# Causal masks as affine selects on GpSimd, with key copies and weight loads reordered, in a fused attention and MLP kernel

## The chip, the cores and the metric

The kernel runs on one core of a Trainium2 chip. The metric is the device time of one execution in microseconds. All profiles are of one execution on that core. The core has TensorE (PE, with its weight loads as PEld), VectorE (DVE), ScalarE (ACT), GpSimd (POOL) and SyncE (SP); loads are issued from the queues of SP, ACT and POOL.

## What is computed

Causal attention with 16 extra "beacon" keys and values that every query sees, for 8 batches and 8 heads of 576 positions and 64 features; then a two-layer network with a leaky ReLU on the 4608 x 512 result.

```
B, H, S, Nb, D = (8, 8, 576, 16, 64)
k_all = concatenate([beacon_k, k], axis=2);  v_all = concatenate([beacon_v, v], axis=2)
scores = 1/sqrt(D) * q @ k_all^T
causal[:, Nb:] = triu(ones((S, S)), k=1)
a = softmax(where(causal, -1e9, scores))
x = (a @ v_all).transpose(0, 2, 1, 3).reshape(B * S, H * D)
h = x @ w_in            # 512 x 2048
out = maximum(0.01 * h, h) @ w_out   # 2048 x 512
```

Inputs and output are fp32; the kernel computes in bf16 with fp32 sums.

## The kernel before, in words

**Units of work.** Two heads make a pair; there are 4 pairs per batch and 32 in all, numbered g. The 592 keys (16 beacons, then 576) lie in 5 chunks of up to 128 rows. For a pair, `score` multiplies key chunks with all queries that may see them, in four parts n = 0 to 3, and ScalarE takes the exponential of each part into a buffer `aT` (keys by queries; three buffers, used by g modulo 3). The score accumulators in PSUM are two, so part n waits until the exponential of part n - 2 has read its own. `masks` then sets to zero what a query may not see: only a triangle in the diagonal block of each chunk. Before the change, it multiplies the block by a 0/1 triangle `tri` on VectorE, in three instructions (lines 326, 333, 339). `value` multiplies `aT` by the values, which carry a column of ones for the row sums, in two halves; VectorE divides by the sums (lines 376, 377). `finish` transposes the result on TensorE, and VectorE copies it into `xT` (line 394).

**The network.** A chunk is 512 of the 4608 rows, so there are 9. `moe1` makes one 128-column slice of the hidden layer of a chunk: 4 matmuls (line 403) and a leaky ReLU on ScalarE (line 410). `moe2` makes a quarter of one output tile: 4 matmuls (line 425), and with the fourth quarter a VectorE copy and a store. Each such set of 4 matmuls is called a group; there are 288. `fill` issues the next group that may be issued: a chunk's first layer once `ready` says that its rows are finished, and second-layer groups in turn with them.

**Keys and queries.** They come in by loads with a cast to bf16, on GpSimd's queue (`load_qk`, 4 loads per half batch, line 149). For batches 0 and 1 (pairs 0 to 7) `t_q` transposes them on TensorE; VectorE copies the queries, ScalarE the keys (line 264; for pair 3 VectorE copies both). The first pair has its own fp32 loads (`load_first_pair`, into a `v_raw` buffer). For batches 2 to 7, `permute` reorders them on GpSimd (line 178), `turn_pairs` transposes them by DMA on SP's queue (line 276), and `in_order` puts them in order on GpSimd (lines 289, 291), one pair ahead. From pair 9 on, an edge added by hand (`behind`) makes `in_order` for pair g + 1 wait for the masks of pair g - 1. Beacon keys are cast by `cast_beacon_k` (line 191), transposed by `beacon_transposes`, and copied in front of each key tile.

**Values.** `load_v` brings a batch in as fp32 on SP's queue (lines 224, 227, 229; two buffers), and `cast_v` casts it on GpSimd, chunk by chunk (line 238).

**Weights.** `load_w_in` and `load_w_out` bring each matrix in with a cast on GpSimd's queue, in four pieces of 512 KB each (bf16), after the loads and casts of batches 0 and 1.

**Order.** The order on each engine is the order of the program's text (`manual_schedule`); nothing is moved by a scheduler. Step g of the main loop issues `loads(g)`, scores of pair g, values of pair g - 2, and `finish(g - 3)`. In steps 0 to 7 the attention of batches 0 and 1 stands alone, with three fills in steps 6 and 7. At g = 8 the rest of these pairs is drained with 27 fills, and from then on each step spreads its share of the remaining groups over eight slots between the attention's parts.

Of the kernel before, what the change touches and what calls it, by code (L numbers as in the profile page):

```python
# [15 lines left out]
def kernel(  # L16
# [66 lines left out]
    tri = singles.tile([128, 128], BF16, name="tri")  # L83

    def make_mask():

        nc.gpsimd.memset(tri, 1.0)
        nc.gpsimd.affine_select(
            out=tri,
            in_=tri,  # L90
            compare_op=ALU.is_ge,
            fill=0.0,
            base=0,
            channel_multiplier=-1,
            pattern=[[1, 128]],
        )
# [25 lines left out]
    def load_w_in(i):  # L122
        return nc.gpsimd.dma_start(
            out=w_in_sb[:, :, i * 512 : (i + 1) * 512], in_=w_in_r[:, :, i * 512 : (i + 1) * 512]
        )

    def load_w_out(i):
        return nc.gpsimd.dma_start(
            out=w_out_sb[:, i * 4 : (i + 1) * 4, :], in_=w_out_r[:, i * 4 : (i + 1) * 4, :]
        )  # L130
# [27 lines left out]
    def load_first_pair():  # L158
        load_beacon_k(0, 1, nc.scalar)
        t = rawpool.tile([128, NKB, H, D], FP32, name="v_raw")  # L160
        flat = t[0:RP].rearrange("p c h d -> p (c h d)")
        n = 2 * RI * D
        for i in range(2):
            first_raw.append(flat[:, i * n : (i + 1) * n].rearrange("p (h i d) -> p h i d", h=2, i=RI))
        for eng, src, dst in zip((nc.sync, nc.scalar), (q, k), first_raw):
            last = eng.dma_start(out=dst, in_=src[0, 0:2].rearrange("h (p i) d -> p h i d", i=RI))
        return last
# [156 lines left out]
    def masks(g):  # L324
        aT = probs[g]
        nc.vector.tensor_tensor(
            out=aT[:, :, 0:112],
            in0=aT[:, :, 0:112],
            in1=tri[:, None, 16:128].to_broadcast([128, 2, 112]),
            op=ALU.mult,  # L330
        )
        diag = aT[:, :, 512 : 512 + 3 * 464].rearrange("p e (c x) -> p e c x", c=3)[:, :, :, 0:128]
        nc.vector.tensor_tensor(  # L333
            out=diag,
            in0=diag,
            in1=tri[:, None, None, :].to_broadcast([128, 2, 3, 128]),
            op=ALU.mult,
        )
        return nc.vector.tensor_tensor(  # L339
            out=aT[0:80, :, 1648:1728],  # L340
            in0=aT[0:80, :, 1648:1728],
            in1=tri[0:80, None, 0:80].to_broadcast([80, 2, 80]),
            op=ALU.mult,
        )
# [94 lines left out]
    done1, done2, ready, turn = [0], [0], [0], [0]  # L439

    def fill():
# [3 lines left out]
        can2 = i2 < NCH and i2 < i1  # L445
# [30 lines left out]
    with order:  # L476
# [4 lines left out]
        load_beacon_k(1, B, nc.sync)  # L481
        load_v(0, after=first)
        load_v(1)
        make_pads()
        make_mask()
        make_ones()
        cast_beacon_k(0, 1, nc.scalar.copy)
        nc.vector.tensor_copy(out=first_cast[0], in_=first_raw[0])
        nc.scalar.copy(out=first_cast[1], in_=first_raw[1])
        cast_beacon_k(1, B, nc.gpsimd.tensor_copy)  # L490
        cast_v(0, nc.gpsimd, 0, 2)
        load_qk(1, 0)
        cast_v(0, nc.gpsimd, 2, 5)
        load_qk(1, 1)
        load_w_in(0)
        cast_v(1, nc.gpsimd, 0, 3)
        load_w_in(1)
        cast_v(1, nc.gpsimd, 3, 5)
        for i in range(2, 4):
            load_w_in(i)  # L500
        for i in range(4):
            load_w_out(i)
        warm_up(34)
        beacon_transposes(0, 1)
# [3 lines left out]


        masked = {}  # L510

        def loads(g):
            b, hp = divmod(g, NPAIR)
            if g == 3:
                load_qk(2, 0)
            elif g == 5:
                load_qk(2, 1)
                for which in range(2):
                    permute(2, 0, which)
                turn_pairs(2, 0)  # L520
            elif g == 7:
                for which in range(2):
                    permute(2, 1, which)
                turn_pairs(2, 1)
                load_v(2)
                in_order(g + 1)
                cast_v(2, nc.gpsimd)
            elif g >= 2 * NPAIR:
                if has(g + 1):
                    copy = in_order(g + 1)  # L530
                    if g > 2 * NPAIR:
                        behind(copy, masked[g - 1])
# [27 lines left out]
        for g in range(NG + 3):  # L560
# [3 lines left out]
            if g < 2 * NPAIR:  # L564
# [5 lines left out]
                if g == 2:  # L570
                    beacon_transposes(1, B)
                if g + 1 < 2 * NPAIR:
                    t_q(g + 1, 0)
                    t_q(g + 1, 1, nc.vector.tensor_copy if g == 2 else nc.scalar.copy)
                if g > 2:
                    value(g - 2, 0)
                if g == 7:
                    fill()
# [4 lines left out]
                if g >= 6:  # L583
                    fill()
                if has(g - 2):
# [4 lines left out]
            if g == 2 * NPAIR:  # L590

                finish(g - 3)
                value(g - 2, 0)
                fill()
                value(g - 2, 1)
                fill()
                finish(g - 2)
                value(g - 1, 0)
                fill()
                value(g - 1, 1)  # L600
                fill()
                fill()
                finish(g - 1)
                for n in range(22):
                    fill()
# [35 lines left out]
            if has(g):  # L641
                masked[g] = masks(g)
# [33 lines left out]
```

## Time and profile before

| | |
|---|---|
| median of 11 runs | 357.91 us |
| lowest and highest | 355.52 and 360.32 us |
| the profiled execution | 357.29 us |
| its span in the profile | 355.6 us |
| mean granted TensorE clock | 0.981 |
| chain that ended last: PE, DMA, POOL | 70%, 15%, 6% |
| ScalarE exponentials (line 320), 128 | 104.3 us busy |
| VectorE masks (lines 326, 333, 339), 96 | 11.1 + 21.2 + 9.1 us busy |
| GpSimd key and query copies (line 291), 48 | 28.4 + 28.3 us busy |

The profile is of one execution. Its page gives the busy time of each engine, then the span in 40 equal slices with one digit of busy share for each, then groups of equal instructions by line: count, busy time, mean duration in ns, and the engine's idle time just ahead of them with what ended it. A line such as `A <- B: 1.3, 2, 0.8` among the waits means that A idled for B, in total 1.3 us, 2 times, at longest 0.8 us. "Granted clock" is the share of full speed that TensorE was given.

### The profile page before, as it was taken

Reading aid. Unit: us, or ns where it says so; the run is one execution under the profiler, and the core shown is the slowest. Engines: PE = TensorE matmul, PEld = TensorE weight load, DVE = VectorE, ACT = ScalarE, POOL = GpSimd, SP = SyncE. Lnnn points to the kernel's source line nnn. Section 1 sums busy time; section 2 is a strip of 40 time slices with the busy share of each in tenths; the row PEclk is TensorE's granted clock in tenths of the full one; section 3 lists DMA queues with packets and bytes.
Section 4 is the critical chain, followed back from the end, with each engine's and each line's share of the span. In section 5 each row is a group of like instructions: output and inputs, shape, how many; then the busy total and the mean of one; then the engine's idle time right before and its main releaser. Section 6 shows DMA issues by size and latency. Waiting matters only on the chain.

```text
span 355.6 us, 7310 instructions
## 1 busy us (share of the span) xinstructions
PE 340.3 (96%) x3002; PEld 172.2 (48%) x3002; DVE 123.5 (35%) x323; ACT 190.9 (54%) x282; POOL 153.3 (43%) x217
## 2 busy tenths in 40 slices
PE   5898899999899999999999999999999999999995
PEld 4476554444454444444444454444444554444444
DVE  2498630133656424322333234323332331000111
ACT  3989754476455873478436843685358304633300
POOL 7555516497698675745474547452220000000000
PEclk9589999999999999999999999999999999999999
DMA  8998999997997884993579355900110011000021
GB/s 163 204 209 134 193 196 193 207 219 122 179 225 130 168 152 107 117 231 54 96 143 225 59 98 95 194 3 0 61 60 2 2 63 55 2 29 29 31 78 71
DMA packets 86929, 40.87 MB, mean 115 GB/s; under 512 B 69872, under 2 KB 82160, under 8 KB 86896
## 3 DMA queue, kind: packets, MB, share of 16 engines
q1 hardware_dynamic: 73456, 26.75, 34.7%
q0 software_dynamic: 13152, 13.34, 25.1%
q10 hardware_dynamic: 288, 0.33, 0.4%
q8 instruction: 23, 0.38, 0.4%
q14 instruction: 10, 0.08, 0.1%
HBM read 37.22 MB, written 9.44 MB: 131 GB/s over the span
## 4 chain that ended last, share of the span: by engine, by line
PE 70%; DMA 15%; POOL 6%; issue 2%; DVE 2%; ACT 2%; SPq 2%; POOLq 0%
PE acc L425 30%; PE acc L403 27%; PE av L367 6%; DMA v_raw<-in_v_dram 6%; PE sc L311 5%; DMA w_out_sb<-in_moe_w_out_dram 4%; DMA q_raw<-in_q_dram 4%; DMA v_raw<-in_k_dram 1%; POOL qT L291 1%; PE tp L389 1%; DVE osb L434 1%; SPq L229 1%; ACT aT L320 1%; POOL kT L291 1%; POOL k_nat L178 1%
## 5 line engine op out<-in xcount | busy, mean ns | idle before, releaser
L403 PE MATMUL acc<-xT,w_in_sb 128*128 128x512 bf16 x576 | 140.2, 379 | 1.4 <-DVE xT L394 1.4
L425 PE MATMUL acc<-w_out_sb,gT 128*128 128x512 bf16 (+1 forms) x592 | 139.6, 374 | 0.0
L320 ACT ACTIVATE aT<-sc 128x1024 bf16<-128x1024 f32 (+3 forms) x128 | 104.3, 870 | 62.1 <-PE sc L311 62.0
L410 ACT ACTIVATE gT<-acc 128x512 bf16<-128x512 f32 x144 | 85.9, 601 | 80.1 <-PE acc L403 80.1
L425 PEld LDWEIGHTS <-gT 128*128 128x128 bf16 x592 | 53.3, 98 | 58.7 <-issue 6.1
L403 PEld LDWEIGHTS <-w_in_sb 128*128 128x128 bf16 x576 | 51.9, 98 | 59.5 <-issue 4.2
L434 DVE COPY osb<-acc 128x512 f32<-128x512 f32 (+1 forms) x37 | 25.1, 677 | 121.4 <-PE acc L425 121.4
L367 PEld LDWEIGHTS <-aT 128*128 128x128 bf16 (+1 forms) x960 | 37.4, 98 | 15.1 <-issue 3.3
L311 PE MATMUL sc<-qT,kT 64*128 64x80 bf16 (+4 forms) x384 | 37.3, 296 | 5.4 <-ACT aT L320 2.5
L367 PE MATMUL av<-v_aug,aT 128*128 128x65 bf16 (+1 forms) x960 | 40.6, 195 | 0.3 <-issue 0.3
L289 POOL COPY kT<-bkT 128x16 bf16<-128x16 bf16 x24 | 4.9, 206 | 63.4 <-DVE aT L339 63.4
L377 DVE TENSOR_TENSOR x_nat<-av,rec 128x384 bf16<-128x384 f32 x64 | 31.4, 491 | 2.2
L376 DVE RECIPROCAL rec<-av 128x6 f32<-128x6 f32 x64 | 12.0, 187 | 57.6 <-PE av L367 57.5
L238 POOL CAST v_aug<-v_raw 128x512 bf16<-128x512 f32 (+1 forms) x40 | 23.8, 629 | 18.0 <-DMA v_raw<-in_v_dram 18.0
L291 POOL COPY kT<-k_turn 128x576 bf16<-128x576 bf16 x24 | 28.4, 1184 | 0.0
L291 POOL COPY qT<-q_turn 128x576 bf16<-128x576 bf16 x24 | 28.3, 1181 | 0.0
L311 PEld LDWEIGHTS <-kT 64*128 64x128 bf16 x384 | 12.9, 96 | 31.3 <-issue 23.0
L394 DVE COPY xT<-tp 128x576 bf16<-128x576 bf16 x32 | 14.5, 453 | 32.8 <-PE tp L389 32.7
L333 DVE TENSOR_TENSOR aT<-aT,tri 128x768 bf16<-128x768 bf16 x32 | 21.2, 661 | 6.2 <-ACT aT L320 6.2
L149 POOL DMA_DIRECT2D k_raw<-in_k_dram x31 | 19.3, 622 | 7.3 <-DMA w_out_sb<-in_moe_w_out_dram 2.9
L149 POOL DMA_DIRECT2D q_raw<-in_q_dram x31 | 19.1, 616 | 6.2 <-PE tp L389 2.3
L178 POOL COPY q_nat<-q_raw 128x1152 bf16<-128x1152 bf16 x12 | 13.9, 1160 | 10.8 <-DMA q_raw<-in_q_dram 10.8
(40 smaller groups left out, 111.2 us busy)
## 6 DMA issues: line engine op xcount, KB each, us to landing
out_dram<-osb SPq DMA_DIRECT2D x35, 256.0 KB, 2.1
v_raw<-in_v_dram SPq DMA_DIRECT2D x24, 256.0 KB, 5.2
q_raw<-in_q_dram POOLq DMA_DIRECT2D x31, 144.0 KB, 5.1
k_raw<-in_k_dram POOLq DMA_DIRECT2D x31, 144.0 KB, 5.3
w_in_sb<-in_moe_w_in_dram POOLq DMA_DIRECT2D x4, 512.0 KB, 8.3
w_out_sb<-in_moe_w_out_dram POOLq DMA_DIRECT2D x4, 512.0 KB, 14.4
v_raw<-in_v_dram SPq DMA_DIRECT2D x8, 224.0 KB, 3.9
v_raw<-in_v_dram SPq DMA_DIRECT2D x8, 160.0 KB, 5.0
```

What stands on the lines that cost most here:

```text
L149: dma = nc.gpsimd.dma_start(out=dst[e * RP : (e + 1) * RP], in_=src[b, h0 : h0 + 2].rearrange("h (p i) d -> p h i d", i=RI),)
L238: eng.tensor_copy(out=dst[0 : ROWS[c], c, :, 0:D], in_=t[0 : ROWS[c], c])
L291: nc.gpsimd.tensor_copy(out=dst.rearrange("c (p i) -> c p i", i=RI), in_=t[:, :, e].rearrange("c i p -> c p i"),)
L311: nc.tensor.matmul(out=sc[:, par, col - c0 : col - c0 + w], lhsT=kT[ps_, c * 128 : (c + 1) * 128], rhs=qT[ps_, q0 : q0 + w], start=True, s ...
L320: nc.scalar.activation(out=aT[:, :, c0 : c0 + w], in_=sc[:, :, 0:w], func=AF.Exp, scale=0.125)
L333: nc.vector.tensor_tensor(out=diag, in0=diag, in1=tri[:, None, None, :].to_broadcast([128, 2, 3, 128]), op=ALU.mult,)
L367: nc.tensor.matmul(out=avv[:, n, 0 : D + 1], lhsT=aT[0 : ROWS[c], par, a0 : a0 + 128], rhs=va[0 : ROWS[c], c, 2 * hp + par, :], start=(c = ...
L377: nc.vector.tensor_tensor(out=x_nat[:, t0:t1].rearrange("p t e d -> p (t e) d"), in0=avv[:, :, 0:D], in1=rec[:, n0:n1, None].to_broadcast( ...
L403: nc.tensor.matmul(out=acc, lhsT=w_in_sb[:, j, fc * 128 : (fc + 1) * 128], rhs=xT[:, j, i * 512 : (i + 1) * 512], start=(j == 0), stop=(j ...
L410: nc.scalar.activation(out=gT[i][:, fc, :], in_=acc, func=AF.Prelu, alpha=0.01)
L425: nc.tensor.matmul(out=acc[:, 0:w], lhsT=gT[i][:, fc, t * 128 : (t + 1) * 128], rhs=w_out_sb[:, fc, c0 : c0 + w], start=(fc == 0), stop=(f ...
L434: nc.vector.tensor_copy(out=osb[:, 0:w], in_=acc[:, 0:w])
```

## The change

The masks become four affine selects per pair on GpSimd, in place on `aT`, and `tri` with its two instructions goes. The copies of the keys of pairs 1, 2 and 4 move from ScalarE to VectorE, so that ScalarE keeps those of pairs 0, 5, 6 and 7. The weights come in halves (1 MB each in bf16): the first layer's in steps 1 and 2, ahead of the second half of batch 1's queries and keys (step 4) and of batch 1's values, which wait until the second half of the first-layer weights has landed. The second layer's halves come within the block of pairs 6 and 7, the last of them ahead of batch 2's values, which wait for its landing. Beacon keys are split 2 + 6 in place of 1 + 7; the six are loaded after batch 0's values, and cast and transposed at the start of the block of pair 6. Steps 0 to 5 hold attention alone. Then a block written out by hand holds what is left of pairs 3 to 7, with 16 first-layer groups, 8 of them at its head; step 7 holds the last `finish`, 8 more groups and the preparation of batch 2. Second-layer groups are held back until step 9. The edge from masks to `in_order` goes.

```diff
     def masks(g):
+
         aT = probs[g]
-        nc.vector.tensor_tensor(
-            out=aT[:, :, 0:112],
-            in0=aT[:, :, 0:112],
-            in1=tri[:, None, 16:128].to_broadcast([128, 2, 112]),
-            op=ALU.mult,
-        )
         diag = aT[:, :, 512 : 512 + 3 * 464].rearrange("p e (c x) -> p e c x", c=3)[:, :, :, 0:128]
-        nc.vector.tensor_tensor(
...
+        for part, base, pattern in (
+            (aT[:, :, 0:112], NB, [[0, 2], [1, 112]]),
+            (diag[:, 0], 0, [[0, 3], [1, 128]]),
+            (diag[:, 1], 0, [[0, 3], [1, 128]]),
+            (aT[0:80, :, 1648:1728], 0, [[0, 2], [1, 80]]),
+        ):
+            nc.gpsimd.affine_select(
+                out=part,
+                in_=part,
+                compare_op=ALU.is_ge,
+                fill=0.0,
+                base=base,
+                channel_multiplier=-1,
+                pattern=pattern,
+            )
...
-    def load_w_in(i):
...
+    def load_w_in(half):
+        cols = slice(half * DF // 2, (half + 1) * DF // 2)
+        return nc.gpsimd.dma_start(out=w_in_sb[:, :, cols], in_=w_in_r[:, :, cols])
+
+    def load_w_out(half):
+        rows = slice(half * NF // 2, (half + 1) * NF // 2)
+        return nc.gpsimd.dma_start(out=w_out_sb[:, rows, :], in_=w_out_r[:, rows, :])
...
-        can2 = i2 < NCH and i2 < i1
+        can2 = second[0] and i2 < NCH and i2 < i1
...
         load_qk(0, 0)
         load_qk(0, 1)
-        load_beacon_k(1, B, nc.sync)
         load_v(0, after=first)
-        load_v(1)
+        load_beacon_k(2, B, nc.sync)
         make_pads()
-        make_mask()
         make_ones()
-        cast_beacon_k(0, 1, nc.scalar.copy)
+        cast_beacon_k(0, 2, nc.scalar.copy)
...
-        cast_v(0, nc.gpsimd, 0, 2)
+        cast_v(0, nc.gpsimd, 0, 1)
         load_qk(1, 0)
-        cast_v(0, nc.gpsimd, 2, 5)
...
+        cast_v(0, nc.gpsimd, 1, 3)
...
+            if g == 1:
+                load_w_in(0)
+                cast_v(0, nc.gpsimd, 3, 5)
+            elif g == 2:
+                load_v(1, after=load_w_in(1))
+            elif g == 4:
+                load_qk(1, 1)
             elif g >= 2 * NPAIR:
-                if has(g + 1):
-                    copy = in_order(g + 1)
-                    if g > 2 * NPAIR:
-                        behind(copy, masked[g - 1])
+                if has(g + 1) and g > 2 * NPAIR:
+                    in_order(g + 1)
...
-                if g + 1 < 2 * NPAIR:
+                if g < 5:
                     t_q(g + 1, 0)
-                    t_q(g + 1, 1, nc.vector.tensor_copy if g == 2 else nc.scalar.copy)
+                    t_q(g + 1, 1, nc.scalar.copy if g == 4 else nc.vector.tensor_copy)
...
+            if g == 6:
+
+                cast_beacon_k(2, B, nc.gpsimd.tensor_copy)
+                cast_v(1, nc.gpsimd, 0, 4)
+                load_qk(2, 0)
+                cast_v(1, nc.gpsimd, 4, 5)
+                beacon_transposes(2, B)
+                finish(3)
+                fill(8)
+                t_q(6, 0)
+                t_q(6, 1, nc.scalar.copy)
+                fill()
+                score(6, 0)
+                score(6, 1)
+                fill()
+                t_q(7, 0)
+                t_q(7, 1, nc.scalar.copy)
+                score(6, 2)
+                score(6, 3)
+                load_w_out(0)
+                masks(6)
+                load_qk(2, 1)
+                value(4, 0)
+                fill()
+                value(4, 1)
+                score(7, 0)
+                score(7, 1)
+                finish(4)
+                fill()
+                value(5, 0)
+                score(7, 2)
+                score(7, 3)
+                masks(7)
+                last = load_w_out(1)
+                value(5, 1)
+                fill()
+                value(6, 0)
+                finish(5)
+                value(6, 1)
+                fill()
+                value(7, 0)
+                finish(6)
+                fill()
+                value(7, 1)
+                fill()
+                continue
+
+            if g == 7:
+                for which in range(2):
+                    permute(2, 0, which)
+                turn_pairs(2, 0)
+                load_v(2, after=last)
+                in_order(8)
+                for which in range(2):
+                    permute(2, 1, which)
+                turn_pairs(2, 1)
+                in_order(9)
+                cast_v(2, nc.gpsimd)
+                finish(7)
+                fill(8)
+                continue
+
+            if g == 9:
+                second[0] = True
```

## The prediction

> **What bounds the kernel now.** I read the page's busy shares and slices first, to see whether one engine is full and where it isn't.
>
> ```profile
> PE 340.3 (96%) x3002; PEld 172.2 (48%) x3002; DVE 123.5 (35%) x323; ACT 190.9 (54%) x282; POOL 153.3 (43%) x217
> ...
> PE   5898899999899999999999999999999999999995
> ...
> PEclk9589999999999999999999999999999999999999
> ```
>
> TensorE is busy nearly throughout and stands idle for 355.6 - 340.3 = 15.3 us. VectorE, which the masks leave, is 35% busy: its load is not the limit as such. The clock row shows a half-speed stretch at the start. Next, the busy time by stretch, to place the 15.3 us (each row: stretch, its length, then busy time of PE, PEld, DVE, ACT, POOL, granted clock, DMA share, GB/s).
>
> ```profile
> 8.80:20.00 11.20, 9.44 (x149) 5.66 (x151) 6.07 (x13) 9.26 (x12) 7.39 (x14) 0.50 1.16 206
> 20.00:31.20 11.20, 10.34 (x254) 7.65 (x249) 10.60 (x32) 10.46 (x14) 2.82 (x6) 0.94 1.14 192
> 31.20:50.00 18.80, 17.08 (x274) 10.79 (x271) 11.74 (x37) 12.96 (x21) 10.04 (x16) 1.00 1.09 169
> 50.00:69.10 19.10, 19.10 (x92) 8.51 (x89) 1.15 (x2) 8.93 (x15) 8.90 (x12) 1.00 1.10 200
> 69.10:85.00 15.90, 15.90 (x100) 6.68 (x100) 5.21 (x10) 12.63 (x18) 11.99 (x17) 1.00 0.98 186
> 85.00:100.00 15.00, 13.72 (x138) 6.79 (x136) 8.44 (x17) 7.61 (x10) 12.04 (x17) 1.00 0.89 168
> 100.00:340.00 240.00, 238.57 (x1879) 115.42 (x1876) 75.04 (x197) 125.68 (x190) 93.74 (x126) 1.00 0.46 89
> ```
>
> Idle TensorE: 4.3 us before 8.8 (start), 1.8 + 0.9 + 1.7 from 8.8 to 50, nothing to 85, 1.3 from 85 to 100, 1.4 in the next 240, 4.0 at the end. So the end is set by how much TensorE work is done when it becomes full, at about 50 us; only about 4.3 + 1.3 us, and the half-clock stretch, can be won. The waits tell what is behind the 1.3 us:
>
> ```profile
> POOL kT L289 <- DVE aT L339: 63.4, 15, 6.8
> ...
> PE sc L311 <- POOL kT L291: 1.3, 2, 0.8
> ```
>
> GpSimd idles 63.4 us for the mask of two pairs back (an edge that the code adds by hand), and TensorE waited 1.3 us for key copies behind it. Last, the prices, by shape:
>
> ```profile
> L333 DVE TENSOR_TENSOR aT<-aT,tri 128x768 bf16<-128x768 bf16 x32 | 21.2, 661 | 6.2 <-ACT aT L320 6.2
> L238 POOL CAST v_aug<-v_raw 128x512 bf16<-128x512 f32 x32 | 19.3, 632 | 17.8 <-DMA v_raw<-in_v_dram 17.8
> L326 DVE TENSOR_TENSOR aT<-aT,tri 128x224 bf16<-128x224 bf16 x32 | 11.1, 345 | 0.0
> L339 DVE TENSOR_TENSOR aT<-aT,tri 80x160 bf16<-80x160 bf16 x32 | 9.1, 286 | 0.0
> L289 POOL COPY kT<-bkT 128x16 bf16<-128x16 bf16 x24 | 4.9, 206 | 63.4 <-DVE aT L339 63.4
> L88 POOL TENSOR_SCALAR_AFFINE_SELECT tri<-tri 128x128 bf16<-128x128 bf16 x1 | 0.3, 290 | 0.1
> ```
>
> **What the skill says.** "GPSIMD Engine Reference", Engine selection: one-input work on GpSimd runs roughly at line rate; no page prices an affine select. The trace agrees for the cast: (632 - 206) / 496 = 0.86 ns per element over a fixed 0.2 us. The same page, Specifications: GpSimd shares SBUF interfaces with VectorE when that reads two SBUF inputs. The trace fits: one L333 mask took 1.60 us at 74.2 beside a GpSimd copy, against 0.55 alone; the change removes that pair. "TensorE: Matmul & The Clock Gate", Part 1: after a window of about 3.4 us without activity the clock halves, and a busy one restores it. Here it fell at 7.7 and rose at 21.3, 13.6 us or four such windows apart. "Trainium Kernel Development and Optimization", Key Constraints: all queues share 16 DMA engines. The trace shows them full (share 1.1) up to 69 us, so that order of loads is all that can be chosen.
>
> **The change, part by part.**
>
> *Masks off VectorE.* 345 + 661 + 286 = 1.29 us per pair, 41 us in all. On the path lies little: TensorE's waits name a mask once, for 0.6 us. *Selects on GpSimd*: per pair 224, 384, 384 and 160 elements. With 0.2 us and 0.86 ns per element: 0.39 + 0.52 + 0.52 + 0.33 = 1.76 us; I take 1.75. Bounds: 4 x 0.29 = 1.16 if length counts for nothing, 1152 / 128 x 0.29 = 2.61 if it is all that counts; below nothing is excluded, since it is added work. *Mask tile*: 1.1 us less on GpSimd under the first loads, hidden there.
>
> *Key copies.* ScalarE's copy (0.64 us) goes to VectorE (0.75) for pairs 1, 2 and 4. Before, a step's ScalarE work was 3.3 (four exponentials, 1.86 + 1.44) + 0.65, and steps came 3.9 us apart. After, VectorE has per step xT 0.45, query 0.76, 0.16, key 0.75, and reciprocals and scalings 0.20 + 0.56 + 0.18 + 0.42: 3.5, with 0.45 idle while TensorE transposes x. So steps come 3.4 apart until values join (step 2), then near 3.5 to 4: first exponentials at 9.2, 12.65, 16.1, then 21.0 (values of pair 0 stand ahead of scores 3 in TensorE's order, half clock), 24.3 and 28.5. Before they stood at 9.4, 13.3, 17.15, 22.15, about 25.7 and 29.4. Last exponential of pair 5: 31.8.
>
> *GpSimd's queue to there* (issues of q/k 0.62 each, of half the weights 0.8): cast 0 to 12.3, four q/k issues 14.7, casts 16.0, masks 0 17.8, first half of the weights 18.6, casts 19.9, masks 1 21.7, second half 22.5, masks 2 24.3, masks 3 26.1, four issues 28.6, masks 4 30.4. Masks 5 wait for 31.8 and end at 33.25; only then comes the cast of the other beacon keys (0.8): 34.05. It is first in TensorE's block of pair 6, and TensorE, done with values 3 at 31.25, waits for it 2.85 us, with ready MoE groups behind it in order. This is a new wait; before, that cast was done at 9.1. The loads don't add to it: seven 512 KB pieces landed 37.4 to 55.2, 3.0 us each, so first weights land near 25, second near 31, batch 1's values behind them near 39.5, cast by 42.5; needed at 46.5. Two waits are new on SP's queue: batch 1's values for the second half (nothing is queued behind them until the transposes of batch 2 near 57), and batch 2's values for the last second-layer half (landing near 62), with the transposes for pairs 10 and 11 behind them; those land near 72 and are read from 75.6. In GpSimd's queue the casts of those values, waiting for SP, hold q/k issues of batch 2 until 41.9 and of batch 3 until 73.8, which I count in the times below.
>
> *Block 6 and 7.* Beacon and x transposes and a wait for xT 34.05 to 35.3; 8 groups at 0.865 (four matmuls of 0.216) 42.2; then 8 groups, scores 6 and 7, values 4 to 7: 59.2 with some 0.6 us of small waits; 8 groups more: 66.4. Scores 8 follow there with 24 groups done. Before they came at 69.1 with 30 done. Six groups are 5.2 us: 66.4 + 5.2 - 69.1 = **+2.5**.
>
> *After that.* The 1.3 us of waits for key copies lose their cause: **-1.3**. But GpSimd now has per step masks 1.75, copies 0.2 + 2 x 1.18, and per batch 4 permutes (4.6), 8 issues (5.0) and 5 casts (3.15): 30 us per batch, against 30 of TensorE's in steps 8 to 11 (6 or 7 groups a step) and 37 later. From its value casts at 71.3 I get key copies for pairs 10 to 13 at 78.2, 88.4, 96.8, 104.4, needed at 80.4, 88.6, 96.2, 104.4: **+0.6**, then more room. If TensorE's wait at 31 empties a clock window, 3.4 us at half speed cost 1.7; where the window falls is open, so half: **+0.85** (ends 0 and 1.7). Moving second-layer groups behind pair 9 costs nothing: the same groups fill later steps.
>
> Sum: 2.5 - 1.3 + 0.6 + 0.85 = +2.65. The profiled execution took 357.29 (355.6 and 1.7 around it), so 359.9; the median shown is 0.6 above it, so **360.6**.
>
> **The rivals.** *Dear selects*: at 2.61 us the queue above ends 3.85 later at the beacon cast, and key copies come 4 x 0.86 = 3.4 later: +7.2, 367.8; at 2.2, 363.8. For it: only one short select is in the trace. Against: the casts' slope. *Steps at ScalarE's pace*, the one that ends on the other side: without the masks and key copies all steps come 3.4 apart, last exponential at 9.2 + 6 x 3.4 = 29.6. The beacon cast then ends 2.2 earlier, and the gap is too short for the clock: 2.65 - 2.2 - 0.85 = -0.4, 357.5. It decides from the beacon transposes starting by 32; if the small waits also go (1.1 us) and selects cost 1.2, it reaches 355. For it: ScalarE is 10.46 of 11.2 busy from 20 to 31; against: VectorE is 10.60 there, and value work stands ahead of scores. *It moves nothing*: the wait at 31 is covered by the earlier arrival; this is the middle of the second rival.
>
> **How the numbers follow.** Forecast 0.47 (own range 358.8 to 363); dear selects 0.13; ScalarE's pace 0.40 (353.5 to 359), half of it faster by over 0.5%. About 0.5% is what a measurement of this kernel can tell from no change. Faster: 0.20. Within: 0.20 + 0.07 from the forecast's low end = 0.27. Slower: 0.53. The range cuts the far ends: 355 to 365.
>
> **What would show it.** A TensorE gap of 2 to 4 us before the six beacon transposes, released by GpSimd; selects adding to about 1.75 us per pair; scores 8 near 66; no waits over 1 us for key copies from 78 to 105; a second half-clock stretch, or none. Wrong if the gap is under 1 us, if exponentials of pair 5 end before 30.5, or if selects take over 2.2 us a pair.

## The result and the profile after

| | before | after |
|---|---|---|
| median, the two measured side by side | 358.44 us (47 runs) | 363.69 us (12 runs) |
| lowest and highest | 355.06 and 360.88 us | 362.22 and 367.33 us |
| the profiled execution | 357.29 us | 363.98 us |
| its span | 355.6 us | 362.1 us |

The ratio of after to before is 1.0165, with a 95% interval from 1.0137 to 1.0193: the change makes the kernel slower by 1.6%. Ratios, here and below, are taken over the fast runs alone (a run over 1.5% above the fastest of its kernel counts as slow) and are not the quotient of the two medians, which is 1.0146 here. The direction is the predicted one and the time lies within 355 to 365 us, but the loss is 1.65% where the forecast had 0.75%, and the time is above the forecast's own range of 358.8 to 363. The profiled executions differ by 6.7 us where the sum said 2.65.

The page of after, the same rows as before:

```profile
PE 345.4 (95%) x3002; PEld 174.3 (48%) x3002; DVE 93.3 (26%) x230; ACT 189.6 (52%) x279; POOL 199.6 (55%) x339
...
PE   6896999699999999999999999999999999999996
...
PEclk9559899999999999999999999999999999999999
```

GpSimd has taken what VectorE lost, and TensorE is still busy 95% of a longer span. Its row has two dents that were not there before, the "6" in the fourth slice (27 to 36 us) and the "6" in the eighth (63 to 72 us). PEclk shows an "8" in the slice behind the first of them; behind the second, a half-speed window of 3.4 us is split over two slices, and the digits hide it. PEclk also has a "5" in the third slice, where before had an "8": in this execution the half-speed stretch at the start lasted from 9.3 to 26.4 us, in the one of before from 7.7 to 21.3. The busy times in the same stretches as before (columns as there):

```profile
8.80:20.00 11.20, 9.88 (x176) 6.61 (x174) 6.10 (x11) 9.68 (x12) 8.17 (x16) 0.52 1.18 197
20.00:31.20 11.20, 10.60 (x191) 7.26 (x188) 7.30 (x21) 8.69 (x11) 9.15 (x21) 0.71 1.11 204
31.20:50.00 18.80, 15.71 (x172) 7.74 (x172) 4.09 (x12) 10.48 (x18) 8.68 (x16) 0.91 0.91 145
50.00:69.10 19.10, 17.43 (x195) 10.02 (x192) 6.67 (x19) 12.31 (x20) 9.34 (x16) 1.00 1.04 147
69.10:85.00 15.90, 14.31 (x73) 5.58 (x74) 0.00 (x0) 10.42 (x16) 15.02 (x23) 0.89 1.17 215
85.00:100.00 15.00, 15.00 (x126) 7.00 (x124) 5.24 (x11) 6.46 (x9) 12.74 (x21) 1.00 0.87 162
100.00:340.00 240.00, 238.58 (x1905) 115.73 (x1904) 57.64 (x140) 126.07 (x190) 131.13 (x216) 1.00 0.47 93
```

From 100 us on the two kernels are alike (238.58 against 238.57 busy): the whole loss is made before. From 85 to 100 the idle time of 1.3 us is gone, as predicted. Most of the loss lies between 31 and 85, where TensorE idles 3.1 + 1.7 + 1.6 us (before: 1.7, 0, 0) and its clock is at 0.91 and 0.89. From 31 to 69 the queues moved 145 and 147 GB/s, where before they moved 169 and 200: loads that were due were not yet issued. From 20 to 31 the clock is at 0.71 against 0.94, the longer stretch at the start. It is worth about 1 us at pair 6 and does not come from the edit: two kernels below run the same program up to there, with half-speed stretches of 13.7 and 10.2 us at the start in place of 17.1, and come to their beacon transposes at 34.0 and 32.9 us instead of 34.9. Places in two profiles with different starts can therefore be compared to within 1 to 2 us only; most of the runs below have 13.7 us there, as before has. The waits of TensorE name two things:

```profile
PE sc L295 <- POOL kT L275: 3.3, 1, 3.3
PE tp L184 <- POOL bk L175: 2.4, 1, 2.4
```

The second is the predicted wait for the beacon cast, from 32.4 to 34.9. The first was not in the prediction: scores of pair 8 wait for their key copies from 67.4 to 70.7. GpSimd's own timeline shows why (columns: start, duration, instruction; in brackets the idle time ahead of it and what ended that):

```profile
54.76 1.72 POOL L318 TENSOR_SCALAR_AFFINE_SELECT aT<-aT 128x224 bf16<-128x224 bf16 x4
56.43 0.90 POOL L114 DMA_DIRECT2D w_out_sb<-in_moe_w_out_dram  x1
57.33 1.16 POOL L162 COPY q_nat<-q_raw 128x1152 bf16<-128x1152 bf16 x1
58.41 1.16 POOL L162 COPY k_nat<-k_raw 128x1152 bf16<-128x1152 bf16 x1
59.50 0.20 POOL L273 COPY kT<-bkT 128x16 bf16<-128x16 bf16 x1
68.27 1.14 POOL L275 COPY qT<-q_turn 128x576 bf16<-128x576 bf16 x1 [8.56 <-DMA q_turn<-q_nat]
69.49 1.15 POOL L275 COPY kT<-k_turn 128x576 bf16<-128x576 bf16 x1
```

The last half of the second-layer weights stands behind the selects of pair 7 and is issued at 56.4. It is 1 MB and landed at 67.3. The transposes for pairs 8 and 9 are issued on SP's queue, that of the queries at 58.5, 2 us after it, and that of the keys at 61.2; they landed at 68.2 and 69.4. Before, with no weights on the way, the first took 3.45 us from issue to landing. So GpSimd stands 8.6 us, and TensorE 3.3 us behind it.

The price of the selects was right (by shape, mean ns of one):

```profile
L318 POOL TENSOR_SCALAR_AFFINE_SELECT aT<-aT 128x384 bf16<-128x384 bf16 x64 | 32.0, 527 | 53.2 <-PE av L349 41.6 <-ACT aT L304 11.6
L318 POOL TENSOR_SCALAR_AFFINE_SELECT aT<-aT 128x224 bf16<-128x224 bf16 x32 | 12.8, 401 | 8.1 <-ACT aT L304 8.1
L318 POOL TENSOR_SCALAR_AFFINE_SELECT aT<-aT 80x160 bf16<-80x160 bf16 x32 | 10.5, 328 | 0.0
```

A set is 0.40 + 2 x 0.53 + 0.33 = 1.78 us (predicted 1.75). The idle time ahead of the selects (61.3 us in all) is time in which GpSimd waits, with everything queued behind; the profile puts its end down to ScalarE's exponentials or TensorE's values.

### The profile page after: what moved, and what is told of

Read it like the earlier page. It is cut to its first block, busy times and chain, and to the rows that moved or that the text cites. A ratio compares the mean times of both kernels' runs of the same rounds, so it can differ in the third digit from the quotient of the medians.

```text
span 362.1 us, 7335 instructions
## 1 busy us (share of the span) xinstructions
PE 345.4 (95%) x3002; PEld 174.3 (48%) x3002; DVE 93.3 (26%) x230; ACT 189.6 (52%) x279; POOL 199.6 (55%) x339
## 4 chain that ended last, share of the span: by engine, by line
PE 81%; POOL 8%; DMA 5%; issue 3%; DVE 2%; ACT 0%; SPq 0%; POOLq 0%
PE acc L407 35%; PE acc L385 31%; PE sc L295 6%; PE av L349 6%; POOL aT L318 3%; DMA q_turn<-q_nat 3%; DMA v_raw<-in_v_dram 1%; DMA v_raw<-in_k_dram 1%; PE tp L371 1%; DVE osb L416 1%; POOL k_raw L133 1%; POOL q_raw L133 1%; POOL v_aug L222 1%; DVE xT L376 1%; POOL w_in_sb L110 0%
## 5 line engine op out<-in xcount | busy, mean ns | idle before, releaser
L304 ACT ACTIVATE aT<-sc 128x1024 bf16<-128x1024 f32 (+3 forms) x128 | 104.3, 872 | 73.9 <-PE sc L295 73.9
L318 POOL TENSOR_SCALAR_AFFINE_SELECT aT<-aT 128x384 bf16<-128x384 bf16 (+2 forms) x128 | 52.7, 446 | 61.3 <-PE av L349 41.6
L385 PEld LDWEIGHTS <-w_in_sb 128*128 128x128 bf16 x576 | 52.5, 99 | 62.9 <-issue 10.1
L349 PEld LDWEIGHTS <-aT 128*128 128x128 bf16 (+1 forms) x960 | 38.5, 100 | 15.6 <-issue 3.0
L295 PE MATMUL sc<-qT,kT 64*128 64x80 bf16 (+4 forms) x384 | 38.3, 302 | 6.2 <-POOL kT L275 3.3
L349 PE MATMUL av<-v_aug,aT 128*128 128x65 bf16 (+1 forms) x960 | 41.4, 197 | 0.0
L371 PEld LDWEIGHTS <-x_nat 128*128 128x128 bf16 (+2 forms) x160 | 11.3, 100 | 7.8 <-DVE x_nat L359 1.3
```

Of the source, the lines that this page charges most:

```text
L295: nc.tensor.matmul(out=sc[:, par, col - c0 : col - c0 + w], lhsT=kT[ps_, c * 128 : (c + 1) * 128], rhs=qT[ps_, q0 : q0 + w], start=True, s ...
L304: nc.scalar.activation(out=aT[:, :, c0 : c0 + w], in_=sc[:, :, 0:w], func=AF.Exp, scale=0.125)
L318: nc.gpsimd.affine_select(out=part, in_=part, compare_op=ALU.is_ge, fill=0.0, base=base, channel_multiplier=-1, pattern=pattern,)
L349: nc.tensor.matmul(out=avv[:, n, 0 : D + 1], lhsT=aT[0 : ROWS[c], par, a0 : a0 + 128], rhs=va[0 : ROWS[c], c, 2 * hp + par, :], start=(c = ...
L385: nc.tensor.matmul(out=acc, lhsT=w_in_sb[:, j, fc * 128 : (fc + 1) * 128], rhs=xT[:, j, i * 512 : (i + 1) * 512], start=(j == 0), stop=(j ...
```

## The theory and how it was tested

Theory: the selects cost little by their own 1.78 us. They cost by where they stand: each set waits for exponentials, and what is behind it in GpSimd's order waits too, including casts and the issue of loads. Two of these hold-ups reach TensorE, the beacon cast at 34 us and the last weights at 56 us, the second by way of transposes that share the DMA engines with a late load. Each wait can also let a clock window fall to half speed. Rivals: the selects cost by themselves; the clock is the main thing; the load order alone, without the selects, loses as much.

A progress mark makes traces comparable: the time at which scores of pair 8 start and the groups of the network done by then. A group is 0.865 us of TensorE at full clock. Before: 69.1 with 30. After: 70.7 with 24, which is 70.7 + 6 x 0.865 - 69.1 = 6.8 us behind.

## The experiments

All ratios are to the kernel before, run beside each, with the 95% interval.

### The two hold-ups taken away, one at a time and together

**Second half of the weights right behind the first** (both issued ahead of the masks of pair 6):

```diff
                 load_w_out(0)
+                last = load_w_out(1)
                 masks(6)
...
                 masks(7)
-                last = load_w_out(1)
```

> The second half of the second-layer weights is issued right behind the first, ahead of the masks of pair 6, instead of just ahead of the DMA transposes for pair 8. Theory (the transposes are late because that 1 MB load stands in the DMA engines beside them): they land 3 to 4 us after issue as in the kernel before, TensorE's wait of 3.3 us before the scores of pair 8 goes, and with it the half-clock window after it (1.7 us): about 5 us less than the changed kernel, ratio to the kernel before near 1.002. Rival (the transposes are late for another reason, such as SP's queue or the q/k loads of batch 2): they still take 8 to 10 us, ratio stays near 1.016.

Measured: 360.58 us, ratio 1.0073 (1.0048 to 1.0098), between the two expectations. The second half landed at 59.2 instead of 67.3, and scores of pair 8 start at 66.9 with 24 groups, 3.8 us earlier than in after (0.9 of it from the shorter half-speed stretch at the start), with a wait of only 0.35 us. But the transposes for pair 8 still took 7.8 us, now beside queries and keys that stand behind the weights and landed at 63.5. The wait of 2.4 us for the beacon cast and one half-speed window behind it (35.8 to 39.2) stay.

**Beacon cast in step 4, ahead of the masks of pairs 4 and 5:**

```diff
             elif g == 4:
                 load_qk(1, 1)
+                cast_beacon_k(2, B, nc.gpsimd.tensor_copy)
...
             if g == 6:
-                cast_beacon_k(2, B, nc.gpsimd.tensor_copy)
```

> The cast of the six beacon keys stands in step 4 on GpSimd, ahead of the masks of pairs 4 and 5, instead of behind them. Theory (TensorE's wait of 2.45 us before the beacon transposes and the half-clock window after it, 1.7 us, come from the order of GpSimd's queue): both go and block 6 runs 4 us earlier. But the transposes for pair 8 hang on loads that don't come earlier, so the scores of pair 8 wait longer, for 5 to 7 us: the sum is 0 to 2 us less than the changed kernel, ratio 1.010 to 1.016. If the two waits were independent, 4 us less, ratio 1.005.

Measured: 361.09 us, 1.0078 (1.0052 to 1.0104), less than the expected 1.010 to 1.016. The wait for the beacon cast is gone, and scores of pair 6 start at 41.2 instead of 46.3 (2.45 us of wait, 1.7 of half-speed window, the rest from the start). TensorE then comes early to pair 8 and waits 2.9 us for its key copies (expected were 5 to 7): scores 8 at 65.1, with a half-speed window from 65.8.

**Both edits.**

> Both moves of the two kernels before this one. Theory (two new waits and the cold windows behind them are the whole loss): no wait over 1 us before the beacon transposes or the scores of pair 8, 9 us less than the changed kernel, ratio 0.990. Rival (GpSimd's fuller queue then holds TensorE from pair 9 on, by key copies): waits for key copies show between 65 and 105 us, ratio 0.995 to 1.005.

Measured: 361.04 us, 1.0084 (1.0051 to 1.0116): no better than either, and slower than both expectations. The wait before pair 8 has grown to 6.3 us and scores 8 start at 68.6. The weights were issued at 45.0 and 45.9 and landed at 56.2 and 62.6; queries and keys of batch 2 landed at 66.3 behind them, and the transposes issued at 53.5 landed at 66.3 too. The two gains are not additive: with the first wait gone TensorE needs the keys earlier, and the loads can't be delivered by then. What was lost between 31 and 50 us, when too few loads had been issued, isn't won back by issuing two of them at once at 45; moving one of the two ahead is the test of this, further below.

### Is it the clock?

Dummy matmuls fill the two waits of after (44 and 56 of them), and change nothing else:

```diff
                 cast_v(1, nc.gpsimd, 4, 5)
+                warm_up(44)
                 beacon_transposes(2, B)
...
                 fill(8)
+                warm_up(56)
                 continue
```

> The changed kernel with 44 and 56 matmuls of 128 columns on the identity, whose result nobody reads, in the two places where TensorE waits (before the beacon transposes, and before the scores of pair 8). The waits stay; only the clock is kept. Theory (each wait empties a clock window, and each half-clock window of 3.4 us costs 1.7): no half-clock stretch after 27 us, 3 to 3.5 us less than the changed kernel, ratio 1.007. If the clock costs nothing there, ratio stays at 1.016.

Measured: 363.51 us (6 runs), 1.0153 (1.0114 to 1.0192), not to be told from after; the 1.007 of the theory is excluded. The clock was full from 21.7 to the end of its profile, so both windows were saved, though 1.3 us of the second wait are left. Scores of pair 9 start at 76.6, 2.9 us earlier than in after, of which up to 1 us is the shorter stretch at the start (pair 5 is already 1.0 us earlier). Then TensorE waits 0.7 and 0.4 us for the key copies of pairs 11 and 12, where after waits for none, and its last instruction ends 1.7 us earlier than there. So of the 3.4 us that two full windows are worth, half at most reaches the end of this profile, since keys are late anyway, and it is too little for the medians to show. The clock is a consequence of the waits and not the main loss.

### The selects without the order, and the order without the selects

**The order of the change, with the VectorE masks of before:**

> The changed kernel with the masks of the kernel before, multiplications by the triangle on VectorE: all of the reordering without the selects. Theory (the selects cost by holding up what stands behind them in GpSimd's queue, casts and the issue of loads, since they wait there for the exponentials): GpSimd then runs ahead, the beacon cast is done near 23 us, all weights are issued by 46, so neither of TensorE's two long waits comes (8 to 9 us with their cold clock windows), while VectorE has 1.3 us more in each of steps 2 to 5 (3 to 5 us): near 358, ratio 0.998 to 1.003. Rival (the reordering itself loses, whoever masks): ratio stays at 1.012 or more.

Measured: 361.04 us, 1.0064 (1.0036 to 1.0092), between the two expectations: part of a loss is there without any select. But it is another loss. GpSimd is free sooner and issues the last weights at 45.3; the transposes issued at 47.4 and 49.7 share the engines with 2 MB of weights and 0.6 MB of queries and keys, and take 13.5 and 16.8 us. Yet TensorE doesn't wait for them: scores of pair 8 start at 68.0 without a wait. From 31 to 57 us its waits are 4.4 us for VectorE, which has masks and moved key copies here, with one half-speed window behind them (49.6 to 53.0):

```profile
PE sc L310 <- DVE aT L325: 1.8, 1, 1.8
PE tp L388 <- DVE x_nat L376: 1.5, 3, 0.7
```

So this run does not say what the load order alone costs.

**Before with only its masks replaced:**

> The kernel before with nothing changed but the masks: selects on GpSimd in place of the triangle. Theory (the same, position in GpSimd's queue decides): the masks of pair 0 stand behind all loads and casts of the start, which end at 38 us, so the values of pair 0 begin near 40 instead of 20 us: 17 to 21 us slower, ratio 1.05 to 1.06. Rival (the selects cost their own busy time only, beside free time of GpSimd): ratio 0.995 to 1.005.

Measured: 387.28 us, 1.0787 (1.0749 to 1.0826); the expectation had 1.05 to 1.06. It shows the mechanism at its plainest, in a wait of TensorE (10 to 50 us) and in GpSimd's timeline:

```profile
PE av L351 <- POOL aT L319: 20.4, 2, 20.2
```

```profile
25.58 0.62 POOL L223 CAST v_aug<-v_raw 128x512 bf16<-128x512 f32 x1 [2.96 <-DMA v_raw<-in_v_dram]
...
31.66 0.62 POOL L223 CAST v_aug<-v_raw 128x512 bf16<-128x512 f32 x1 [4.77 <-DMA v_raw<-in_v_dram]
34.58 0.61 POOL L223 CAST v_aug<-v_raw 80x512 bf16<-80x512 f32 x1 [2.30 <-DMA v_raw<-in_v_dram]
35.14 1.48 POOL L108 DMA_DIRECT2D w_in_sb<-in_moe_w_in_dram  x2
36.60 2.98 POOL L113 DMA_DIRECT2D w_out_sb<-in_moe_w_out_dram  x4
39.55 4.73 POOL L319 TENSOR_SCALAR_AFFINE_SELECT aT<-aT 128x224 bf16<-128x224 bf16 x12
```

In the order of before, the casts of batch 1's values and all weight loads are in GpSimd's order ahead of the first masks. On VectorE the masks did not mind; as selects they stand behind casts that wait for loads, and TensorE waits 20.2 us for the mask of pair 0. It waits once more, 8.4 us up to 76.1, for the selects of pair 7, which stand behind the casts of batch 2's values, and these wait for loads; the expectation had left that one out. So the reordering of loads is no extra of the change: the selects need it.

**Before, with selects from pair 8 on**, VectorE masks for pairs 0 to 7, and without the edge by hand:

> The kernel before with VectorE's masks for pairs 0 to 7 and selects from pair 8 on, and without the edge from masks to key copies. In these steps the loads stand ahead of the masks in each step already. Theory (1.6 us of selects per pair fit into GpSimd's free time there): TensorE's waits for key copies shrink from 1.3 us or stay, ratio 0.995 to 1.000. Rival (selects crowd out the key copies): waits for key copies of 2 us or more between 75 and 105, ratio over 1.005.

Measured: 359.73 us, 1.0030 (1.0002 to 1.0058). The theory's gain didn't come; the rival's 1.005 lies inside the interval, but the waits for key copies that it needs (2 us or more) didn't come either, they are 0.9 us in all. Its profile has two half-speed windows from 33.9 to 40.7, after a TensorE wait of only 1.2 us and ahead of any changed instruction; it is 3.1 us behind before at pair 8 (72.2 against 69.1 with 30 groups each) and 2.9 us behind at its end. So in this profile the selects cost nothing from pair 8 on, and gain nothing.

### Does the load delay the transposes?

In these two kernels the second half of the weights is issued behind the key copies of pair 8, at 61 to 62 us; in the first the beacon cast stays where the change put it, in the second it is early, in step 4:

```diff
                 masks(7)
-                last = load_w_out(1)
...
-                load_v(2, after=last)
+                load_v(2)
                 in_order(8)
+                load_w_out(1)
```

> The changed kernel with one edit: the second half of the second-layer weights is issued behind the key copies of pair 8, and batch 2's values no longer wait for it; the beacon cast stays behind the masks of pair 5. Theory (the transposes for pair 8 were late since that load was under way): they land within 5 us of their issue, the 3.3 us wait before scores 8 and the half-speed window behind it go, the wait before the beacon transposes stays at 2 to 3 us; scores 8 near 66 to 67.5; some of it comes back as waits for the key copies of pairs 9 and 10, beside the moved load; ratio 1.006 to 1.011. Rival (the transposes are late for another reason, such as the late issue of queries and keys): scores 8 stay at 70 or later, ratio 1.014 or more.

> The beacon cast early as in the second kernel; and the second half of the second-layer weights is issued behind the key copies of pair 8, with the values of batch 2 no longer waiting for it. In all five kernels that have the hand-written block, the transposes for pair 8 landed within 1.2 us of the last load ahead of them on GpSimd's queue. Theory (they get little of the DMA engines while a large load of that queue is under way): with the queue empty near 56 us they land by 59, the scores of pair 8 come without a wait at 62 to 63; later waits for key copies of pair 10 of up to 3 us remain: near 357.5, ratio 0.994 to 1.000. Rival (SP's queue is late of itself): they still take 8 us or more, ratio near 1.008.

Measured: 362.07 us, 1.0111 (1.0073 to 1.0149) for the first and 359.91 us, 1.0032 (1.0007 to 1.0056) for the second. In time the first can't be told from after (1.0137 to 1.0193); what it shows is in the trace. The transposes of after and of the first, by tile:

```profile
L260 SPq DMA_TRANSPOSE q_turn<-q_nat x2: 1965/2274/2583, 58.5 to 72.0; - x2
...
DMA to landing us min/median/max: 4.2/7.0/9.7
```

```profile
L260 SPq DMA_TRANSPOSE q_turn<-q_nat x2: 1923/2123/2323, 55.3 to 63.8; - x2
...
DMA to landing us min/median/max: 3.3/6.7/10.1
```

The extremes have changed places. In after it is the first (58.5, with the load under way) that takes 9.7 us; with the load moved, the first takes 3.3 us and the second (63.8, pairs 10 and 11), now beside the load, takes 10.1. Scores of pair 8 start at 65.0 without a wait; instead TensorE waits 2.8 us for the keys of later pairs. In the second they start at 63.8 without a wait, and later waits for keys come to 3.9 us, where up to 3 were expected; the ratio is above the expected 0.994 to 1.000. The same for the other kernels (us; the load of GpSimd's queue that was issued before the transpose and landed last, and the landing of the first transpose, that of the queries):

| kernel | transpose issued | that load landed | transpose landed |
|---|---|---|---|
| after | 58.5 | 67.3 (weights) | 68.2 |
| weights right behind | 56.7 | 63.5 (keys) | 64.5 |
| beacon cast early | 53.4 | 62.2 (weights) | 62.8 |
| both | 53.5 | 66.3 (keys) | 66.3 |
| changed order, VectorE masks | 47.4 | 65.8 (weights) | 61.0 |
| weights last, pair 8 | 55.3 | 56.8 (keys) | 58.6 |
| weights last, pair 10 | 63.8 | 72.7 (weights) | 73.9 |

In all rows but one the transpose lands with the load or up to 1.8 us behind it. "DMA: Bandwidth & Descriptors" of the Trainium skill, under Queues, rings and completion order, says that a DMA engine takes turns between the queues that have work for it, packet by packet. The trace agrees while both move. In the run with both edits, from 58 to 62 us (queue, packets, MB, share of the engines; q0 is GpSimd's queue, q1 SP's, with the transposes):

```profile
q0 software_dynamic: 616, 0.62, 91.9%
q1 hardware_dynamic: 614, 0.16, 30.1%
```

As many packets pass on one queue as on the other, but those of the load carry 1 KB and those of the transposes 256 bytes, so the transposes get a fifth of the bytes. The one exception fits this: in the changed order with VectorE masks the transposes shared the engines from 51.5 us on, long enough to be done before the load. A second part of the delay lies ahead of the sharing and stays open: in after no packet passes on SP's queue from 58.5 to 62 us, and the first of a transpose comes at 63.0, 4.5 us after its issue, where before it came after 1.3.

### A version without the hold-ups

If the theory is whole, the changed kernel with its loads issued in time should lose nothing. Beacon cast in step 4, first half of the weights behind the first value cast of batch 1, second half where the first stood:

```diff
...
-                cast_v(1, nc.gpsimd, 0, 4)
+                cast_v(1, nc.gpsimd, 0, 1)
+                load_w_out(0)
+                cast_v(1, nc.gpsimd, 1, 4)
...
-                load_w_out(0)
+                last = load_w_out(1)
                 masks(6)
...
                 masks(7)
-                last = load_w_out(1)
```

> The changed kernel, selects kept; the cast of the six beacon keys stands in step 4, and both halves of the second-layer weights are issued earlier on GpSimd: the first behind the first value cast of batch 1 (near 37 us), the second ahead of the masks of pair 6 (near 44 us), where the first half stood. Theory (what the change lost is hold-ups in GpSimd's order: loads issued late, and transposes that share the DMA engines with a late load): the second half lands by 57 us, transposes for pair 8 land by 60, no wait over 1 us for key copies before pair 8 and none before the beacon transposes, scores 8 at 63.5 to 65.5 with 24 groups; ratio 0.993 to 1.002. Rival (the selects themselves cost, wherever the loads are): ratio 1.005 or more with those waits gone. Second rival (the DMA engines are full, so the load only moves another wait): values of batch 1 or queries and keys of batch 2 come late, a wait of 2 us or more shows in the block of pairs 6 and 7 or before pair 8, ratio 1.004 to 1.010.

Measured: 356.33 us (22 runs) beside 358.64 of before: ratio 0.9960 (0.9938 to 0.9981), as expected, and faster than both kernels. The stretches from 31 to 85:

```profile
31.20:50.00 18.80, 18.37 (x234) 9.97 (x231) 6.46 (x18) 14.54 (x24) 12.64 (x24) 1.00 1.12 190
50.00:69.10 19.10, 19.10 (x160) 9.72 (x158) 3.89 (x12) 13.10 (x23) 13.83 (x20) 1.00 1.17 204
69.10:85.00 15.90, 15.83 (x113) 6.84 (x111) 3.34 (x7) 7.95 (x11) 13.73 (x24) 1.00 0.93 167
```

TensorE idles 0.4 + 0 + 0.1 us, the clock is full, and the queues move 190 and 204 GB/s. The weights were issued at 36.2 and 42.7 and landed at 46.3 and 55.0, the transposes for pair 8 at 59.0 and 60.2; scores of pair 8 start at 62.4 with 24 groups, which is 1.5 us ahead of before and 8.3 us ahead of after. (The expectation had said 63.5 to 65.5.) The selects are all still on GpSimd. Beside the run with both edits the program differs in one thing only, the place of the first half of the weights, which is issued at 36.2 instead of 45.0. That alone takes the ratio from 1.0084 to 0.9960, with intervals far apart.

**The same order with VectorE masks:**

> The same order of loads and casts as in the run with both halves ahead, but with the masks of before on VectorE (and their tile). Theory: with the hold-ups gone the selects cost next to nothing, so this is within 0.4% of that run; 0.992 to 1.002 against before. Rival (selects cost by themselves): this is 0.5% or more faster than that run.

Measured: 358.44 us, 1.0014 (0.9988 to 1.0040). That is 0.5% slower than with the selects, and the two intervals don't overlap, so the rival fell; the difference is also larger than the theory's 0.4%, and in favour of the selects: in this order they are better than the masks. TensorE's waits from 31 to 66 us, first with the masks, then with the selects:

```profile
PE tp L388 <- DVE x_nat L376: 2.1, 4, 1.0
PE acc L402 <- DVE xT L393: 1.0, 1, 1.0
```

```profile
PE tp L371 <- DVE x_nat L359: 0.2, 1, 0.2
PE acc L385 <- DVE xT L376: 0.2, 1, 0.2
```

With masks on VectorE, the scalings and copies of finished rows come later from it, and TensorE idles 3.1 us for them instead of 0.4. The difference of 2.7 us is of the size of that between the two medians (2.1 us). One more thing differs in these profiles: with the masks the first weights were issued 0.2 us ahead of the last part of batch 1's values, which took 10.2 us to land; no wait of TensorE shows it.

### The key copies alone

Before, with the key copies of pairs 1, 2 and 4 on VectorE as well:

```diff
-                    t_q(g + 1, 1, nc.vector.tensor_copy if g == 2 else nc.scalar.copy)
+                    t_q(g + 1, 1, nc.vector.tensor_copy if g < 4 else nc.scalar.copy)
```

> The kernel before with only the key copies of pairs 1, 2 and 4 on VectorE. By the prediction's step (ScalarE's 3.3 us of exponentials then set the pace of the first steps) pairs 1 to 4 start 0.5 us earlier each and the start of pair 5 comes 1 to 2 us earlier; half of that reaches the end: ratio 0.995 to 0.999. Rival (VectorE, with masks and key copies, sets the pace): no earlier, ratio 1.000 to 1.004.

Measured: 357.95 us, 0.9980 (0.9948 to 1.0012): inconclusive in time. In the profile pairs 1 to 3 start 1.2 to 1.4 us earlier than before, pairs 4 and 5 0.5 us, pairs 6 and 7 not at all (33.4 and 37.7 in both). Pair 0, whose copies are the same in both, is itself 0.45 us earlier, so nothing is left of the gain at pair 5, where 1 to 2 us were expected.

## Where the prediction failed: right in sign, short in size

Up to 67 us the timetable held within 1 us, in part by luck. *Selects*: 1.78 us a set for 1.75; the rival of dear selects fell. *Exponentials and the beacon cast*: the cast ended at 34.8, predicted 34.05; TensorE waited 2.45 us for 2.85, with beacon transposes at 34.9. The rival of ScalarE's pace, which needed them by 32, fell. *Block of pairs 6 and 7*: TensorE had done what stands ahead of scores 8 at 67.4, predicted 66.4. Three errors nearly cancel in this: the beacon transposes came 0.8 us late, about what the longer half-speed stretch at the start is worth; a half-speed window (36.6 to 40.0), worth 1.7, fell inside the block, which the prediction counts apart; and without it the block took 30.9 us where 32.35 were counted, 1.5 less. (The count has 0.3 us more from 59.2 to 66.4 than its eight groups come to.)

With six groups fewer done that is 67.4 + 5.2 - 69.1 = +3.5 us, window included; the prediction had +2.5 and half a window, +3.35 in all. *Key-copy waits of 85 to 100 us*: -1.3, as predicted, but that they came from the edge is not shown: the run with selects from pair 8 on has no edge either and still waits 0.9 us for key copies. *Key copies late by GpSimd's load*: predicted +0.6; no wait for them from 78 to 105, so 0.

The step that failed is "Scores 8 follow there with 24 groups done". It took the key copies of pair 8 to be in time. Behind it is a mis-sized term, the last second-layer half "landing near 62": it landed at 67.3, since it was issued only at 56.4, behind the selects of pair 7. The prediction listed what waits for that load on SP's queue (batch 2's values, and pairs 10 and 11 behind them), but not what merely runs beside it: the transposes for pairs 8 and 9, queued ahead of those values, for which it names no time at all. The first took 9.7 us where it had taken 3.45 before. That adds a wait of 3.3 us, and behind the wait came a second half-speed window (70.8 to 74.2), 1.7 us of work.

The sum with what was measured: 3.5 - 1.3 + 0 + 3.3 + 1.7 = 7.2 us; TensorE's last instruction ends 7.0 us later than before (358.6 against 351.6), and the profiled times differ by 6.7. It is an account of this one profile, with about 1 us of the start in it, and not of what each term is worth alone: with both windows saved, 3.4 us in the sum, the time hardly moved.

Was it foreseeable? The profile of before showed the DMA share at 1.1 up to 69 us, and the prediction quoted "Trainium Kernel Development and Optimization", Key Constraints, on the 16 shared engines. It used this for the order of loads and not for the duration of the transposes in their midst. The runs with the weights last and with the weights ahead confirm that part in their traces: when the weights aren't beside the transposes for long, these land in 3.3 us (weights last), or 1.1 us behind the keys ahead of them (weights ahead), and the wait is gone.

*VectorE's relief* was priced at nearly nothing ("TensorE's waits name a mask once, for 0.6 us"; that line stands for three waits of weight loads, of 0.2 us each). In the order with the weights ahead it is worth 0.5%, as waits for finished rows that masks had pushed back, not waits for masks. That is a second step of the prediction that was too small, on the other side; what it is worth in after was not measured.

What stays open: the single edits and both together are within their intervals of each other (1.0073, 1.0078, 1.0084), so how much of the loss belongs to which hold-up can't be split; why a transpose beside a load is so late with its first packet; and why the clock fell behind a wait of 1.2 us in one profile and not behind waits of 1.7 in others.

## What to carry to other kernels

Before work is moved to an engine whose order also holds load issues, follow each load behind it: when it is issued now, when it lands, and which transfers on other queues will then run beside it; give those up to the load's remaining time and not their usual one. A wait in such an order is dear by what is queued behind it, so issue the loads first and the waiting work after; here the same selects are 1.6% slower than before or 0.4% faster, by the place of one cast and two loads. And when one wait is taken away, check that what comes next is there earlier too, or the next wait takes the gain.

## What was not expected of the hardware

- A DMA transpose that takes 3.3 us with no large load under way took 7 to 17 us beside one of 1 MB, in packets of 256 bytes against 1 KB and turn by turn. Its issue on SP's queue is slower too: 2.6 and 5.7 us for the two of pair 8 in after, 1.9 and 1.3 with the load moved.
- TensorE's clock fell for one window of 3.4 us after each wait of 2.4 to 3.3 us that wasn't filled (twice in after, once each with the weights right behind, with the beacon cast early and with the weights last), and for two after the wait of 6.3. After waits of 1.7 it did not fall (the two kernels with the weights last), after one of 1.8 (changed order with VectorE masks) and the one of 1.2 it did. "TensorE: Matmul & The Clock Gate", Part 1, puts the fall after an idle window of about 3.4 us; here waits shorter than that were enough, some of them followed by transposes and not by large matmuls.
- An affine select of 384 elements a partition (128 partitions, bf16) takes 0.53 us, of 224 0.40, and of 160 on 80 partitions 0.33: from 224 to 384 elements 0.79 ns per element, over a fixed 0.22 us.
